# Multi-query attention with a SiLU feed-forward on one core: K of two chunks in two column tiles, two query blocks by the whole array at the loop's start, and another tail

## The chip, the cores and the metric

One core of one Trainium2 chip. TensorE (PE) multiplies, with the weights loaded beside it (PEld); VectorE (DVE), ScalarE (ACT) and GpSimd (POOL) do the element work; SyncE (SP) issues most transfers. Time is the device's, in microseconds, for one execution. The kernel before took 1090.62 us (median of three, 1089.78 to 1091.57).

## The reference

Inputs are 2048 tokens of width 512. 32 query heads of width 16 share one K and one V of width 16. Beside the attention stands a feed-forward of width 1792, and a gate mixes them:

```
q = (x @ wq) in 32 heads;  k = x @ wk;  v = x @ wv
a = softmax(q k^T / 4) v, heads joined, @ wo
b = silu(x @ w1) @ w2
g = sigmoid(sum(x * gate_w))
out = g * a + (1 - g) * b
```

## The kernel before, in words

Each fp32 operand is kept as two fp16 parts (a "split": one copy on ScalarE or VectorE, one subtraction on VectorE), and a product is three matmuls. The first pass does all the work at fixed scales; checks along the way fill `mxs`, and a second, slower pass runs only if a flag is set, which it is not here.

**Prologue** (`first_pass`). The instructions of each engine stand in the order in which the code issues them (a manual schedule), so a late operand holds everything behind it on that engine. `T(c, t)` transposes 128 tokens of chunk c (four matmuls against the identity into a bank `pt`) and splits them into `xs`; there are four chunks of 512 tokens. `K(c)` makes K, V and the gate's sum of one chunk in one bank (twelve matmuls with 64 weight columns). `parts`, `v_rows`, `place`, `V` copy K, keep its largest value, put K into the layout `KT`, and turn V. `W` splits wq, `Q(n)` makes query block n (n = 4 x chunk + o, 128 query columns each) and writes it to DRAM (`qd`), `load_q` reads it back into a tile `qb`, `shift` bounds its scores through `kab` and writes the softmax's shift (`sh`). Query blocks 0 and 1 are made here (`AHEAD` is 2). `Pieces` splits the 37 pieces of w1, wq, w2 and wo, each loaded by a DMA into one of three raw tiles; `step` does one piece.

**Loop** (`attention`). 32 rounds (16 query blocks, two halves each) of 16 key tiles make 512 steps; an iteration takes two steps, s and s + 1. A string of letters says what PE does in it: S is one of four groups of scores (line 977, eight matmuls on 50 rows by 32 columns) followed by one exponential on ScalarE (line 980, 128 x 1024); F is one slot of the product stream; P and N are probabilities times V. In the first of the two steps the probabilities may be split (PPP, with VectorE's two subtractions at line 1001) or native fp32 (N); `low` decides that by `split_step`; the other step is always native. Six F stand in an iteration, twelve in a `WIDE` one, which is taken after a tanh while `debt` is 6 or more.

The product stream (`stream`, `outs`) makes, out by out, the hidden layer (`ffn_h`, whose eviction is a tanh), the later query blocks (`q_block`), the second layer (`ffn_o`) and the output projection (`out_proj`). An out's upper 64 rows of products run beside the lower 64 rows of the next out: a slot holds four 64 x 32 products of each. Banks come from `pM`, of which there are two.

`fill` closes an iteration: from a budget in microseconds less what was spent, it issues work that was put off (`todo`), a weight piece, or a chore. After the last query bound (`open_q` empty), chores gather the checks: `gather` writes `md` to DRAM, `row` reads it back on SP, `check` (line 634) works on it.

**Tail.** After the loop, `plain` sends what is left of the stream through the whole array, 128 x 128, in order, two banks, each out evicted when it is done.

Of the kernel before, what the change touches and what calls it, by code (L numbers as in the profile page):

```python
# [28 lines left out]
FIRST = "SSBSSFFFFFF"  # L29
AHEAD = 2  # L30
# [14 lines left out]
def kernel(  # L45
# [158 lines left out]
    nc.gpsimd.memset(mxs, 0.0)  # L204
    for q in qb_:
        nc.gpsimd.memset(q, 0.0)
    for t_ in (VH, VL, VF):
        nc.gpsimd.memset(t_, 0.0)
    nc.gpsimd.memset(VH[:, :, 16:17], 1.0)
    nc.gpsimd.memset(VF[:, :, 16:17], 1.0)  # L210

    def masks(cst):
# [4 lines left out]
        mj = cst.tile([16, 8, 16], F32)  # L217
        nc.gpsimd.iota(mj, pattern=[[0, 8], [1, 16]], base=0, channel_multiplier=-1, allow_small_or_imprecise_dtypes=True)
        sel_k = cst.tile([16, 8, 16], F32)
        nc.vector.tensor_scalar(flat(sel_k), flat(mj), 0.0, None, op0=OP.is_equal)  # L220
        selA = cst.tile([16, 8, 16], F16)
        selB = cst.tile([16, 8, 16], F16)
        nc.vector.memset(selA, 0.0)
        nc.vector.memset(selB, 0.0)
        for b in (0, 2, 4, 6):
            nc.vector.tensor_copy(selA[:, b], sel_k[:, b])
        for b in (1, 5):
            nc.vector.tensor_copy(selB[:, b], sel_k[:, b])
        part = cst.tile([128, 1], F32)
        nc.gpsimd.iota(part, pattern=[[0, 1]], base=0, channel_multiplier=1, allow_small_or_imprecise_dtypes=True)  # L230
        pm = cst.tile([128, 1], F32)
        nc.vector.tensor_scalar(pm, part, 64.0, -64.0, op0=OP.is_ge, op1=OP.mult)
        nc.vector.tensor_tensor(pm, pm, part, op=OP.add)
        rm = cst.tile([128, 2], F32)
# [5 lines left out]
        hj = cst.tile([128, 32], F32)  # L240
        nc.gpsimd.iota(hj, pattern=[[16, 32]], base=0, channel_multiplier=0, allow_small_or_imprecise_dtypes=True)
# [6 lines left out]
        return sel_k, selA, selB, m_one, hmask  # L248
# [35 lines left out]
    def loads(sb, q_cols):  # L284

        wkr = sb.tile([128, KD, DH], F32)
        nc.scalar.dma_start(wkr, by_row(wk))
        wvr = sb.tile([128, KD, DH], F32)
        nc.scalar.dma_start(wvr, by_row(wv))
        gwr = sb.tile([128, KD], F32)  # L290
        nc.scalar.dma_start(gwr, gate_w.rearrange("(p k) -> p k", k=KD))
        xn = []
        for c in range(NCH):
            t_ = sb.tile([128, 4, D], F32, name=f"xn{c}")
            for a in range(2):
                nc.sync.dma_start(t_[:, 2 * a:2 * a + 2], x[c * 512 + a * 256:c * 512 + a * 256 + 256].rearrange("(t p) d -> p t d", p=128))
            xn.append(t_)
        wqr = sb.tile([128, KD, q_cols], F32)
        nc.sync.dma_start(wqr, by_row(wq)[:, :, :q_cols])
# [4 lines left out]
        nc.gpsimd.tensor_copy(flat(wkv[:, :, 48:49]), gwr)  # L304
        return xn, wqr, wkv
# [17 lines left out]
    def sigmoid(sb, pv_, zsc):  # L323

        ez = sb.tile([128, NKT, 1], F32)
        nc.scalar.activation(ez, pv_[:, :, 16:17], AF.Exp, scale=zsc)
        ez = flat(ez)
        nc.vector.tensor_scalar(ez, ez, 1.0, None, op0=OP.add)
        nc.vector.reciprocal(gg, ez)
        nc.vector.tensor_scalar(g1, gg, -0.5, 0.5, op0=OP.mult, op1=OP.add)  # L330
# [20 lines left out]
    def first_pass():  # L351
        with ExitStack() as pro:
# [3 lines left out]
            sel_k, selA, selB, m_one, hmask = masks(sb)  # L356
            xn, wqr, wkv = loads(sb, 256)
            pieces_ = Pieces(S1, S2, SO, SQ)
            bank = lambda name, bufs: ps.tile([128, 512], F32, name=name, bufs=bufs)
            wkvs = sb.tile([128, 2, KD, 64], F16)  # L360
            vr = sb.tile([64, S], F32)
            mx = sb.tile([16, NCH], F32)
            mxa = sb.tile([16, 1], F32)
# [7 lines left out]
            def K(c):  # L371
                ks[c] = bank("pk", 2)
                kv_product(ks[c], wkvs, c)

            def parts(c):
                pk = ks[c]
                k1, k2 = ks[c, "k"] = [wk_.tile([16, 512], F16, name=n) for n in ("k1", "k2")]
                nc.scalar.activation(k1, pk[0:16], AF.Copy, scale=k_to)
                absmax(mx[:, c:c + 1], k1)
                if c == NCH - 1:  # L380
                    nc.vector.tensor_reduce(mxa, mx, axis=AX.X, op=OP.max)
                nc.vector.scalar_tensor_tensor(k2, pk[0:16], k_to, k1, op0=OP.mult, op1=OP.subtract)

            def v_rows(c):
                nc.scalar.activation(vr[32:64, c * 512:c * 512 + 512], ks[c][32:64], AF.Copy)

            def place(c):
                pk = ps.tile([128, 512], F32, name="pt", bufs=4)
                k_places(pk, *ks[c, "k"], selA, selB)
                nc.scalar.activation(KT[:, c * 512:c * 512 + 512], pk, AF.Identity, bias=m_one)  # L390

            def V(c):
                for t in range(4 * c, 4 * c + 4):
                    nc.tensor.transpose(pv_[:, t], vr[32:64, t * 128:t * 128 + 128], ident[32:64, 32:64])
# [20 lines left out]
            def shift(n, pu):  # L415
# [4 lines left out]
                if n == 0:  # L420

                    for p, queue in enumerate((nc.scalar, nc.sync)):
                        queue.dma_start(qb_[0][48:113:64, p], s1[32 * p:32 * p + 3:2])
                return q_shift(o, c, s1)

            split(wkvs[:, 0], wkvs[:, 1], wkv, SKV)
            for m, a, n in (M_K, 0, 16), (M_V, 32, 16), (M_G, 48, 1):
                absmax(mxs[:, m:m + 1], wkvs[:, 0, :, a:a + n], AX.XY)
            T(0, 0, 1, 2, 3)

            pq = bank("pq", 1)
            pv_ = ps.tile([128, NKT, 32], F32, name="pv")
            T(1, 0, 1)
            K(0)
            T(1, 2, 3)
            T(2, 0)
            parts(0)
            T(2, 1)
            v_rows(0)
            K(1)  # L440
            place(0)
            T(2, 2, 3)
            T(3, 0)
            V(0)
            parts(1)
            T(3, 1)
            v_rows(1)
            W(0)
            W(1)
            K(2)  # L450
            pieces_.step(by_scalar=True)
            pieces_.step(by_scalar=True)
            place(1)
            T(3, 2, 3)
            V(1)
            parts(2)
            for _ in Q(0, pq):
                pass
            load_q(qb_[0], 0, 0, 0, 0)
            v_rows(2)  # L460
            pieces_.step(by_scalar=True)
            K(3)
            parts(3)
            place(2)
            q1 = Q(1, bank("pq", 1))
            next(q1)
            prep = bank("pk", 2)
            nc.tensor.matmul(prep[:, 0:1], flat(sel_k), mxa, start=True, stop=True)
            kv_ = sb.tile([128, 1], F32)
            nc.vector.tensor_copy(kv_, prep[:, 0:1])  # L470
            nc.vector.tensor_scalar(kab, hmask, kv_, 2.0 ** -10 * (1 + 2.0 ** -9), op0=OP.mult, op1=OP.mult)
            v_rows(3)
            place(3)
            note = shift(0, bank("pk", 2))
            pieces_.step(by_scalar=True)
            V(2)
            V(3)
            nc.vector.tensor_copy(VF[:, :, 0:16], pv_[:, :, 0:16])
            v_parts()
            sigmoid(sb, pv_, -1.0 / (SX * SKV))  # L480
            nc.vector.tensor_scalar(g1, g1, 1.0 / (SX * S1 * S2), None, op0=OP.mult)
            nc.vector.tensor_scalar(gg, gg, 1.0 / (SX * SKV * SO), None, op0=OP.mult)

            lo = sb.tile([16, 2], F32)
            nc.vector.tensor_scalar(lo[:, 0:1], mxa, 0.5, None, op0=OP.is_lt)
            nc.vector.tensor_scalar(lo[:, 1:2], mxa, 6e4, None, op0=OP.is_gt)
            nc.vector.tensor_tensor(mxs[0:16, M_KK:M_KK + 1], lo[:, 0:1], lo[:, 1:2], op=OP.max)
# [3 lines left out]
            pieces_.step(by_scalar=True)  # L491

        with ExitStack() as phase:
            attention(phase, lambda c, o: DH ** -0.5 / LAM, 0.5 / (SX * S1), 1, pieces_, list(chores()),
                      list(range(AHEAD, NO * NCH)), [(1, 0, qx)])


    def second_pass():
        with ExitStack() as pro:
# [3 lines left out]
            sel_k, selA, selB, m_one, hmask = masks(sb)  # L503
# [80 lines left out]
            sigmoid(sb, pv_, zsc)  # L584
# [13 lines left out]
        with ExitStack() as phase:  # L598
            phase.enter_context(tc.manual_schedule())
            attention(phase, lambda c, o: esc[:, c * NO + o:c * NO + o + 1], tsc, 2, pieces_, [], [], [])  # L600
# [95 lines left out]
    def attention(ctx, scale_of, t_scale, shifts, split_pieces, chores, q_todo, bounds):  # L696
# [55 lines left out]
        def fill(length):  # L752
# [3 lines left out]
            if bounds and turn[0] and turn[1] == 6 and not turn[0].hidden and len(bounds) > turn[0].is_q:  # L756
# [5 lines left out]
            if split_pieces.left() and (room >= 1.3 or split_pieces.count < 6.6 + 0.6 * cycle[0]):  # L762
# [44 lines left out]
        queue, open_q = [], q_todo + bounds  # L807

        def q_block(n):
# [4 lines left out]
            def evict(pq):  # L814
                q2 = qx.rearrange("p (a b) -> p a b", a=2)
# [3 lines left out]
                qa = wp.tile([128, 512], F32, name="e", bufs=2).bitcast(F16)  # L819
# [287 lines left out]
```

## Time and profile before

| what | us |
|---|---|
| median of three runs | 1090.62 |
| the profiled execution | 1091.79 |
| its span | 1089.8 |
| first score matmul | 41.05 |
| first exponential | 42.84 |
| end of the last exponential | 1068.55 |
| end of the last sum on VectorE | 1084.15 |
| PE / ACT / DVE busy | 1065.3 / 1012.0 / 792.9 |

A row of the timeline has start, duration, engine, line, operation, the tiles written and read, count, and in brackets how long the engine sat idle before it and for whom. A row of the view by stretches has the stretch, its length, the engine's busy time with the instructions touched in brackets, the granted TensorE clock (1.00 is full), the share of the DMA engines and GB/s. A row of a group has its count, its busy time and the mean in ns, and the idle time before.

### The profile page before, as it was taken

How to read it: one execution, taken by the hardware profiler on the slowest of the kernel's cores; microseconds unless marked ns; L12 is line 12 of the kernel's file. 1: busy time of each engine (PE TensorE's matmuls, PEld its weight loads, DVE VectorE, ACT ScalarE, POOL GpSimd, SP SyncE). 2: the span in 40 equal slices, each digit the busy share in tenths (PEclk: the TensorE clock that was granted, in tenths of full speed). 3: DMA queues.
4: the chain of work that ended last, by engine and by line, in shares of the span. 5: the costliest groups of instructions: out<-in, count | busy, mean ns of one | idle time of the engine just before them, and what ended most of it. 6: DMA issues, size and time to landing. Idle time of an engine off the chain costs nothing.

```text
span 1089.8 us, 66260 instructions
## 1 busy us (share of the span) xinstructions
PE 1065.3 (98%) x31366; PEld 700.0 (64%) x31366; DVE 792.9 (73%) x1085; ACT 1012.0 (93%) x1123; POOL 23.5 (2%) x53
## 2 busy tenths in 40 slices
PE   7999999999999999999999999999999998999996
PEld 5355666767665577677755667587756775656652
DVE  5647886978779687878776696776868657675875
ACT  4699999999999999999999999899999998999992
POOL 1110000000000000000000000000000000000000
PEclk9799999999999999999999999999999999999999
DMA  5221211210001000000000100000000101000001
GB/s 205 84 64 38 69 42 40 60 34 21 12 11 40 31 22 7 18 12 11 22 11 21 36 28 12 21 12 12 22 5 20 50 11 21 12 9 7 12 4 43
DMA packets 20841, 32.97 MB, mean 30 GB/s; under 512 B 5137, under 2 KB 12050, under 8 KB 20562
## 3 DMA queue, kind: packets, MB, share of 16 engines
q1 hardware_dynamic: 17614, 20.46, 6.0%
q0 software_dynamic: 2512, 8.13, 2.6%
q8 instruction: 247, 4.05, 1.6%
q14 instruction: 32, 0.26, 0.1%
q10 hardware_dynamic: 436, 0.07, 0.0%
HBM read 20.12 MB, written 8.52 MB: 26 GB/s over the span
## 4 chain that ended last, share of the span: by engine, by line
PE 87%; DVE 7%; ACT 4%; DMA 1%; issue 1%; ACTq 0%; SPq 0%; POOL 0%
PE pv L1023 34%; PE pm L736 31%; PE S L977 19%; ACT P L980 4%; DVE L L1001 3%; DMA md<-raw 1%; PE pm L740 1%; PE pt L310 1%; DMA gwr<-in_gate_w_dram 1%; DVE acc L717 0%; DVE T L924 0%; PE pk L124 0%; PE pk L125 0%; PE pk L126 0%; DVE U L925 0%
## 5 line engine op out<-in xcount | busy, mean ns | idle before, releaser
L980 ACT ACTIVATE P<-S 128x1024 f32<-128x1024 f32 x1024 | 965.6, 1047 | 31.3 <-PE S L977 22.3
L977 PE MATMUL S<-qb,KT 50*32 50x512 f16 x8192 | 491.3, 379 | 2.5 <-ACT P L980 2.5
L1001 DVE TENSOR_TENSOR L<-P 128x1024 f16<-128x1024 f32 x352 | 412.2, 1217 | 10.5 <-ACT P L980 10.4
L1023 PE MATMUL pv<-P,VF 64*32 64x512 f32 x5376 | 377.2, 591 | 0.0
L977 PEld LDWEIGHTS <-KT 50*32 50x32 f16 x8192 | 191.5, 90 | 183.7 <-issue 120.8
L736 PE MATMUL pm<-w2s,H 64*32 64x512 f16 x5184 | 262.1, 375 | 3.8 <-issue 2.7
L736 PE MATMUL pm<-xs,w1s 64*32 64x512 f16 x5376 | 247.6, 377 | 1.0 <-DVE acc L717 0.6
L736 PEld LDWEIGHTS <-H 64*32 64x32 f16 x5184 | 148.9, 93 | 43.8 <-issue 16.3
L736 PEld LDWEIGHTS <-w1s 64*32 64x32 f16 x5376 | 143.0, 93 | 39.8 <-issue 12.7
L1023 PEld LDWEIGHTS pv<-P,VF 64*32 64x32 f32 x5376 | 130.9, 107 | 26.8 <-issue 9.5
L785 DVE SCALAR_TENSOR_TENSOR e<-e,pm 128x512 f32<-128x512 f32 x56 | 38.4, 685 | 141.1 <-ACT e L784 140.0
L736 PE MATMUL pm<-xs,wqs 64*32 64x512 f16 x1344 | 93.2, 375 | 0.0
L1023 PE MATMUL pv<-L,VH 64*32 64x512 f16 x1408 | 84.9, 375 | 0.7 <-DVE L L1001 0.5
L1023 PE MATMUL pv<-P,VH 64*32 64x512 bf16 x1408 | 84.7, 389 | 0.0
L1023 PE MATMUL pv<-P,VL 64*32 64x512 bf16 x1408 | 84.2, 386 | 0.0
L1023 PEld LDWEIGHTS <-VH 64*32 64x32 f16 x2816 | 66.5, 92 | 20.9 <-issue 6.0
L736 PE MATMUL pm<-wo_s,O 64*32 64x512 f16 x1440 | 65.9, 375 | 0.0
L924 DVE STREAM_TRANSPOSE T<-pv 128x512 f32<-128x512 f32 x32 | 22.9, 717 | 54.1 <-PE pv L1023 43.5
L736 PEld LDWEIGHTS <-wqs 64*32 64x32 f16 x1344 | 49.1, 93 | 12.7 <-issue 4.1
L717 DVE SCALAR_TENSOR_TENSOR acc<-pm,g,acc 128x512 f32<-128x512 f32 x48 | 35.7, 744 | 25.3 <-PE pm L736 23.2
L736 PEld LDWEIGHTS <-O 64*32 64x32 f16 x1440 | 34.3, 93 | 13.2 <-issue 2.4
L784 ACT ACTIVATE e<-pm 128x512 f32<-128x512 f32 x56 | 34.4, 615 | 6.3 <-PE pm L736 6.3
(148 smaller groups left out, 491.1 us busy)
## 6 DMA issues: line engine op xcount, KB each, us to landing
qb<-qd SPq DMA_DIRECT2D x192, 32.0 KB
raw<-in_B_w_dram POOLq DMA_DIRECT2D x23, 256.0 KB, 3.0
xn<-in_A_x_dram SPq DMA_DIRECT2D x8, 512.0 KB
out_dram<-acc SPq DMA_DIRECT2D x16, 256.0 KB
qd<-qx SPq DMA_DIRECT2D x14, 256.0 KB
raw<-in_A_wo_dram POOLq DMA_DIRECT2D x4, 256.0 KB, 2.9
qb<-sh SPq DMA_DIRECT2D x62, 2.0 KB
raw<-in_B_w_dram SPq DMA_DIRECT2D x3, 256.0 KB
```

Source lines behind the costliest of these rows:

```text
L310: nc.tensor.transpose(pt[:, kt], xn[c].rearrange("p t (d k) -> p t k d", k=KD)[:, t, kt], ident)
L717: nc.vector.scalar_tensor_tensor(a, po, gate[:, n:n + 1], a, op0=OP.mult, op1=OP.add)
L736: nc.tensor.matmul(self.bank[32 * m:32 * m + 32], l(i, rows, 32 * m), r(j, rows), start=first, stop=last)
L740: nc.tensor.matmul(self.bank, l(i, slice(0, 128), 0, 128), r(j, slice(0, 128)), start=first, stop=last)
L784: nc.scalar.activation(e, ph, AF.Tanh, scale=t_scale)
L785: nc.vector.scalar_tensor_tensor(e, e, 1.0, ph, op0=OP.add, op1=OP.mult)
L924: nc.vector.transpose(T, pv[0])
L977: nc.tensor.matmul(sc[32 * m:32 * m + 32, f], KT[b:b + 50, k0:k0 + 32], qtile[i][b:b + 50, j], start=True, stop=True)
L980: nc.scalar.activation(P[:, 2 * j:2 * j + 2], sc, AF.Exp, scale=scale_of(c, o))
L1001: nc.vector.tensor_tensor(lows[s][:, q], P[:, q], upper(P)[:, q], op=OP.subtract)
L1023: nc.tensor.matmul(pvs[i][h][32 * j:32 * j + 32], a[r], b[r, j], start=first, stop=last)
```

## The change

`K(c)` now makes chunks c and c + 1 together: each of its twelve products is issued twice, into PSUM partitions 0 to 63 and 64 to 127 of one bank. So `parts`, `vr`, the masks and the maximum work on 80 or 128 partitions and twice instead of four times; `V` turns 128 x 128. The identity is made first, the clearing of tiles on POOL comes after the loads, wq is loaded before the last chunk. The prologue's order is new, its weight pieces are two instead of five on ScalarE, and the gates' VectorE part moves into iteration s = 4. This is ScalarE's queue from its start to the loop (`xs` are splits of transposed tokens, `wkvs` of the K, V and gate weights, `KT` is K in place, `qs_` a query block, `w1s` a weight piece). Before:

```order
L115 ACTIVATE wkvs<-wkv 128x256
L115 ACTIVATE xs<-pt 128x4x128 x9
L378 ACTIVATE k_287<-pk 16x512
L115 ACTIVATE xs<-pt 128x4x128
L385 ACTIVATE vr<-pk 32x512
```

Now:

```order
L116 ACTIVATE xs<-pt 128x4x128 x4
L116 ACTIVATE wkvs<-wkv 128x256
L116 ACTIVATE xs<-pt 128x4x128 x8
L116 ACTIVATE wqs<-wqr 128x2x256 x2
L394 ACTIVATE k_321<-pk 80x512
L395 ACTIVATE vr<-pk 128x512
L116 ACTIVATE xs<-pt 128x4x128 x4
L116 ACTIVATE qs__367<-pq 128x512
```

Four token splits now stand ahead of the weights' split, and twelve ahead of the first K copy (ten before).

In the loop, the first iteration has no F. Its string FIRST has 28 letters, and E is one whole-array matmul of query blocks 4 and 5 (`EARLY`): ten before the first scores, fourteen between them. Those two blocks leave the list of the stream. Each is followed by a weight piece. `split_step` asks for a VectorE backlog under 0.8, `fill` hands out pieces at 0.57 an iteration from 5.6 (0.6 from 6.6 before), `debt` starts at 18, and bounds are taken in the order of their blocks, no longer beside a query block's end. This moves the check's read on SP. Before:

```order
L623 DMA md<-raw_80 128x1
L256 DMA qb_83<-qd_3_107 16x2x512
L257 DMA qb_83<-qd_3_107 16x2x512
L258 DMA qb_83<-qd_3_107 16x2x512
L260 DMA qb_83<-sh_3_108 1x2x512
...
L628 DMA raw_81<-md 1x128
```

Now:

```order
L649 DMA md<-raw_80 128x1
L654 DMA raw_81<-md 1x128
L262 DMA qb_84<-qd_3_91 16x2x512
```

The read of `md` stood behind the eight loads of a query tile, and now stands right behind the write; on VectorE three hidden-layer evictions lie between the gather and the check.

In the tail, 18 of the 36 whole-array products of before now lie in the stream. What is left, one `ffn_o` and four `out_proj`, goes into banks that are free by then (two of the scores' tiles are used), the four out by out in turn. VectorE's queue from the last probabilities on. Before:

```order
L931 TENSOR_TENSOR C<-T,rr 128x16x16
L935 STREAM_TRANSPOSE T<-C 128x512
L119 CAST O<-T 128x512
L120 TENSOR_TENSOR O<-T,O 128x512
L717 SCALAR_TENSOR_TENSOR acc<-pm,g_65,acc 128x512
L717 SCALAR_TENSOR_TENSOR acc<-pm,gg,acc 128x512 x4
L717 SCALAR_TENSOR_TENSOR acc<-pm,g_65,acc 128x512 x3
```

Now:

```order
L965 TENSOR_TENSOR C<-T,rr 128x16x16
L743 SCALAR_TENSOR_TENSOR acc<-pm,g_65,acc 128x512
L969 STREAM_TRANSPOSE T<-C 128x512
L120 CAST O<-T 128x512
L121 TENSOR_TENSOR O<-T,O 128x512
L743 SCALAR_TENSOR_TENSOR acc<-S,g_65,acc 128x512
L743 SCALAR_TENSOR_TENSOR acc<-pm,gg,acc 128x512 x2
L743 SCALAR_TENSOR_TENSOR acc<-S,gg,acc 128x512 x2
```

Five sums follow O instead of eight, and one stands ahead of the last transpose (row 841 of VectorE's order).

The diff, cut to its core:

```diff
-FIRST = "SSBSSFFFFFF"
-AHEAD = 2
+FIRST = "EEEEEEEEEESEESEEEESEEEESEEEE"
+AHEAD, EARLY = 2, (4, 5)
...
             def K(c):
-                ks[c] = bank("pk", 2)
-                kv_product(ks[c], wkvs, c)
+                pk = ks[c] = bank("pk", 2)
+                for kt in range(KD):
+                    for n, (i, j) in enumerate(((0, 0), (0, 1), (1, 0))):
+                        for h in range(2):
+                            nc.tensor.matmul(pk[64 * h:64 * h + 64], wkvs[:, i, kt], xs[:, j, kt, (c + h) * 512:(c + h) * 512 + 512],
+                                             start=kt + n == 0, stop=kt == KD - 1 and n == 2)
+                    yield
...
-                    for p, queue in enumerate((nc.scalar, nc.sync)):
-                        queue.dma_start(qb_[0][48:113:64, p], s1[32 * p:32 * p + 3:2])
+                    for p in range(2):
+                        nc.sync.dma_start(qb_[0][48:113:64, p], s1[32 * p:32 * p + 3:2])
...
+            T(0, 0, 1, 2, 3)
             split(wkvs[:, 0], wkvs[:, 1], wkv, SKV)
+            pq = bank("pq", 2)
+            T(1, 0, 1, 2, 3)
+            T(2, 0, 1)
+            k = K(0)
+            next(k)
+            next(k)
+            T(2, 2)
+            next(k)
+            next(k)
+            T(2, 3)
+            W(0)
+            W(1)
+            parts(0)
+            T(3, 0)
+            q0 = Q(0, pq)
+            next(q0)
+            next(q0)
+            T(3, 1)
+            next(q0)
+            next(q0)
+            T(3, 2, 3)
+            next(q0)
+            load_q(qb_[0], 0, 0, 0, 0)
+            place(0)
+            place(1)
+            V(0)
+            k = K(2)
+            for _ in k:
+                pass
+            parts(2)
...
-            if bounds and turn[0] and turn[1] == 6 and not turn[0].hidden and len(bounds) > turn[0].is_q:
+            if bounds and turn[0] and turn[1] == 6 and not turn[0].hidden and not turn[0].is_q:
...
-            if split_pieces.left() and (room >= 1.3 or split_pieces.count < 6.6 + 0.6 * cycle[0]):
+            if split_pieces.left() and (room >= 1.3 or split_pieces.count < 5.6 + 0.57 * cycle[0]):
...
-            return steps[s][1] > 0 and not (turn[0] and turn[0].hidden and (0 < turn[1] <= 6 or wide[0]))
+            return steps[s][1] > 0 and backlog[0] < 0.8 and not (turn[0] and turn[0].hidden and (0 < turn[1] <= 6 or wide[0]))
...
+        def early_products():
+            for n in early:
+                o = q_block(n)
+                o.bank = pM.tile([128, 512], F32, name="pm")
+                for i in range(len(o.mm)):
+                    o.whole(i, i == 0, i == len(o.mm) - 1)
+                    if i < len(o.mm) - 1:
+                        yield
+                o.evict(o.bank)
+                split_pieces.step()
+                yield
...
+            if gates_ and s == 4:
+                gates_()
+                spend(0.6)
...
         plain[0] = True
+        for _ in work:
+            pass
+        bank = lambda: pM.tile([128, 512], F32, name="pm")
+        halves = lambda: (lambda t: [t[:, 0], t[:, 1]])(pS.tile([128, 2, 512], F32, name="S"))
...
+        ends, banks = [], halves()
+        while left[0]:
+            o = next(seq)
+            if o is not None:
+                o.bank = banks.pop(0) if banks else bank()
+                whole([o], range(len(o.mm)))
+                ends.append(o)
         while todo:
             todo.pop(0)[2]()
-        for _ in work:
-            while todo:
-                todo.pop(0)[2]()
+        for o in ends[:1]:
+            o.evict(o.bank)
+        outs_ = [o() for o in urgent]
+        for o, b in zip(outs_, [bank(), bank()] + halves()):
+            o.bank = b
+        whole(outs_, range(2))
+        whole(outs_, range(2, 3 * NO))
+        for o in outs_ + ends[1:]:
+            o.evict(o.bank)
```

More of the change, by code (lines that the diff above doesn't have):

```diff
@@ L375, in parts @@
             def parts(c):
                 pk = ks[c]
[L377 to L385, printed above, removed]
+                k1, k2 = ks[c, "k"] = [wk_.tile([80, 512], F16, name=n) for n in ("k1", "k2")]
@@ new lines, in first_pass @@
+            V(0)
[3 more added lines that the diff above has]
+            parts(2)
+            pieces_.step(by_scalar=True)
+            q1 = Q(1, bank("pq", 2))
+            next(q1)
+            next(q1)
+            prep = bank("pk", 2)
+            nc.tensor.matmul(prep[:, 0:2], flat(sel_k[0:80]), mxa, start=True, stop=True)
+            kv_ = sb.tile([128, 1], F32)
+            nc.vector.tensor_reduce(kv_, prep[:, 0:2], axis=AX.X, op=OP.max)
+            nc.vector.tensor_scalar(kab, hmask, kv_, 2.0 ** -10 * (1 + 2.0 ** -9), op0=OP.mult, op1=OP.mult)
@@ L427, in first_pass @@
+            next(q1)
+            note = shift(0, bank("pk", 2))
+            place(2)
+            place(3)
+            pieces_.step(by_scalar=True)
             for m, a, n in (M_K, 0, 16), (M_V, 32, 16), (M_G, 48, 1):
                 absmax(mxs[:, m:m + 1], wkvs[:, 0, :, a:a + n], AX.XY)
[L429 to L475, printed above, removed]
-            V(2)
-            V(3)
-            nc.vector.tensor_copy(VF[:, :, 0:16], pv_[:, :, 0:16])
+            lo = sb.tile([128, 2], F32)
+            nc.vector.tensor_scalar(lo[:, 0:1], kv_, 0.5, None, op0=OP.is_lt)
+            nc.vector.tensor_scalar(lo[:, 1:2], kv_, 6e4, None, op0=OP.is_gt)
+            nc.vector.tensor_tensor(mxs[:, M_KK:M_KK + 1], lo[:, 0:1], lo[:, 1:2], op=OP.max)
@@ L502, in second_pass @@
             ps = pro.enter_context(tc.tile_pool(name="props", bufs=2, space=PSUM))
-            sel_k, selA, selB, m_one, hmask = masks(sb)
+            identity(sb)
+            sel_k, selA, selB, m_one, hmask, _ = (t[0:16] if n < 3 else t for n, t in enumerate(masks(sb)))
             xn, wqr, wkv = loads(sb, D)
@@ L827, in bound @@
         def bound():
-            o, c, qa = bounds.pop(0)
+            o, c, qa = bounds.pop(min(range(len(bounds)), key=lambda n: bounds[n][1] * NO + bounds[n][0]))
+            shifted.add((o, c))
             ahead.append(next(seq))
@@ L849, in outs @@
                 else:
-                    for _ in range(2):
+                    while any((k - 1, f) not in Hs for f in range(GF[blocks[k - 1][1]])):
                         yield urgent.pop(0)() if urgent else None
@@ L869, in follow @@
             return o
-        seq, ahead, ended, debt = outs(), [], [None], [12]
-        drains = [0]
+        seq, ahead, ended, debt = outs(), [], [None], [18]
+        drains, left = [0], [4 * len(blocks)]
         turn = [None, 0]
@@ L1045, in attention @@
                 slots, order = NATIVE, [(s - 2, 3), (s - 1, 3)]
-            if not s and bounds:
+            if not s and early:
                 slots = FIRST
@@ L1058, in attention @@
                     n_f += 1
-                elif a == "B" and (bound_now() or not s and bounds):
+                elif a == "B" and (bound_now() or s == 4 and bounds):
                     bound()
```

163 lines of the change are left out of this document (98 added, 65 removed).

## The prediction

> **What bounds the kernel now.** The page first: TensorE (PE) is busy for nearly the whole span.
>
> ```profile
> span 1089.8 us, 66260 instructions
> PE 1065.3 (98%) x31366; PEld 700.0 (64%) x31366; DVE 792.9 (73%) x1085; ACT 1012.0 (93%) x1123; POOL 23.5 (2%) x53
> ```
>
> 98% is not 98% of useful work, so I cut the span at the exponentials of line 980, four to a loop iteration. The view by stretches, for that line alone, gives iteration lengths (second column: us; in brackets the exponentials touched).
>
> ```profile
> 42.84:55.47 12.63, 7.84 (x9) 0.59 0.29 85
> 55.47:1064.70 1009.23, 953.88 (x1013) 1.00 0.08 24
> 241.19:244.91 3.72, 3.72 (x6) 1.00 0.04 11
> 77.15:81.26 4.11, 3.75 (x5) 1.00 0.20 62
> 149.70:153.65 3.95, 3.84 (x4) 1.00 0.02 5
> 175.50:180.69 5.19, 3.99 (x5) 1.00 0.20 58
> 132.81:137.54 4.73, 4.01 (x6) 1.00 0.35 118
> 915.67:923.27 7.60, 3.84 (x6) 1.00 0.26 23
> ```
>
> Row by row: the first two iterations take 12.63 us; the next 253 take 1009.23; a split iteration is 3.72, a native one 4.11 with a tanh and 3.95 without, a wide native one 5.19. The last two are outliers, 1.0 and 3.6 us over their kind. PE explains the kinds. Eight 64-row by 32-column products share one slot, 24 of them start 0.65 us before the next kind (0.217 a slot); behind them, from the chain of waits, a split PV (0.67) and a native one (0.86):
>
> ```profile
> 72.94 0.84 PE L736 MATMUL pm<-xs,w1s 64*32 64x512 f16 x24
> 73.59 0.38 PE L977 MATMUL S<-qb,KT 50*32 50x512 f16 x2
> ```
>
> ```profile
> 65.97 0.67 PE pv L1023 x22
> 66.86 0.86 PE pv L1023 x16
> ```
>
> Four score slots, six product slots, a split PV and a native PV make 3.70. So an ordinary iteration is bound by PE at full clock and cannot be shortened without taking slots away. What can go lies before 55.47, in the outliers, and behind the last exponential. The granted clock shows the first of these (stretches of 3.41 us, PE alone; the third number from the right is the clock):
>
> ```profile
> 37.36:40.77 3.41, 3.41 (x10) 0.50 0.37 102
> 40.77:44.18 3.41, 1.58 (x28) 1.00 0.22 83
> 44.18:47.60 3.42, 2.92 (x44) 0.50 0.63 169
> 47.60:51.01 3.41, 3.41 (x48) 0.50 0.13 44
> 51.01:54.42 3.41, 3.41 (x44) 0.50 0.00 0
> ```
>
> The half clock comes back behind a stretch of 1.58 us of work, and stays while products with one half missing leave part of the array unused; four slow stretches lie around the loop's start.
>
> **The prologue, to the first exponential (now 42.84).** Its rows:
>
> ```profile
> 4.91 3.66 PE L310 MATMUL pt<-ident,xn 128*128 128x128 f32 x16 [4.91 <-DMA xn<-in_A_x_dram]
> 7.77 0.42 ACT L115 ACTIVATE wkvs<-wkv 128x256 f16<-128x256 f32 x1 [4.23 <-POOL wkv L304]
> L116 DVE SCALAR_TENSOR_TENSOR xs<-pt,xs 128x512 f16<-128x512 f32 x13 | 8.5, 683 | 6.8 <-ACT xs L115 6.8
> L382 DVE SCALAR_TENSOR_TENSOR k<-pk,k 16x512 f16<-16x512 f32 x4 | 2.7, 668 | 0.0
> 32.58 0.33 SPq L409 DMA_DIRECT2D qd<-qs__415  x1
> 37.80 1.36 ACTq L423 DMA_DIRECT2D qb<-s  x1
> 41.05 0.62 PE L977 MATMUL S<-qb,KT 50*32 50x512 f16 x16
> 42.32 0.61 ACT L192 ACTIVATE w1s<-raw 128x512 f16<-128x512 f32 x1
> ```
>
> The input still sets 4.9, so the earlier identity gives nothing. K now costs 48 slots of 0.217 us (10.4 us). In column tiles of 64 two chunks share a slot: 24 slots, 5.2 us saved if they run side by side, nothing if not. No row shows 64-column tiles paired; the nearest is the eight-tile row above, which does run side by side, so I take 5.2 and keep 0 as the other end. The transposes move ahead of the wkvs activation, which held ScalarE until 7.77.
>
> Step by step for the new order: ten groups of transposes at the cold 0.92 us each (3.66/4) end at 14.1; K 2.6 and three groups of 0.55 at 18.3; VectorE, at 0.68 a split, is through with wqs only at 19.5 to 20.2, so the first Q block runs 19.5 to 22.8 with a group in it and two more groups end at 23.9; its write leaves at 25.8 instead of 32.58, and the q loads behind it as much earlier. Places and V 1.5, K 2.6: 27.9. Then ScalarE's copy 0.6, VectorE's maximum and k2 (0.67 each) and four short ones (some 0.7) to kab, the bound and its shift 1.1: 31.7, and two SP issues of 0.65 in place of ScalarE's 1.36: 33.2, usable 1.9 us later (37.80 + 1.36 to 41.05), 35.1. PE meanwhile has the Q1 remainder, places and V to 33.3, and ten slots of early blocks, 2.15: scores at 35.5, first exponential at 35.9. ScalarE is free by 35.3: it issues no late DMA and converts two weight pieces instead of five, the last of which (42.32) holds 42.84 today. Places where PE thins out (18.3 to 19.5, 29.2 to 31) can bring a half-clock stretch, up to 1.7 us each; I add 0.6. **36.5, a gain of 6.3**; bounds 35.0 (clock up one stretch sooner) and 39.5 (two slow stretches more).
>
> The Trainium skill, "TensorE: Matmul & The Clock Gate" (Part 4), says a transpose does not count as PE work for the clock. Transposes fill the new prologue's first 9 us, so by that rule the clock would come up some 2 us later than I take it. No row here decides it: the clock came up only after K had begun.
>
> **The loop's first two iterations (12.63).** Now PE does there only half-empty slots (one half of a product with no partner). New: 4 score slots and 14 early whole-array slots, 3.9 us, and one native iteration, 3.95. The change of tile shape costs about 0.1 us, from the pitch across it (0.32 from the first row to the second; 0.22 within one shape):
>
> ```profile
> 20.09 0.38 PE L126 MATMUL pk<-xs,wkvs 128*64 128x512 f16 x1
> 20.41 0.39 PE L320 MATMUL pt<-k,selA 16*128 16x512 f16 x1
> 20.63 0.37 PE L321 MATMUL pt<-k,selB 16*128 16x512 f16 x1
> ```
>
> The first iteration changes shape eight times: 0.8. Sum 8.65; one half-clock stretch at even chance adds 0.85. **9.5, a gain of 3.1**; bounds 8.0 and 12.
>
> The Trainium skill, "TensorEngine Tiling (Array Packing)" (Key Properties), says that a change of tiling mode drains the array, and speaks against this mixing; a full drain at each change (0.38 of a product less its 0.22 slot) would make 1.3 of the 0.8.
>
> **The other 253 iterations (1009.23).** The two blocks leave the stream (24 slots) and 18 products of the tail enter it. By the order of both programs, split 160 becomes 153, native 63 becomes 73, wide split 14 becomes 11 (a wide native's 5.19 less the 0.19 between the PVs: 5.0), wide native stays 16: -7 x 3.72 + 10 x 4.0 - 3 x 5.0 = -1.0, which I leave as spare. The outliers matter more. The check's read of md stands behind eight q loads on SP and VectorE waits for it; in the new order nothing stands between:
>
> ```profile
> 923.73 0.37 SPq L628 DMA_DIRECT2D raw<-md  x1
> 925.07 0.37 DVE L634 TENSOR_REDUCE raw<-raw 1x32 f32<-1x128 f32 x1 [4.76 <-DMA raw<-md]
> 133.33 0.84 PE L736 MATMUL pm<-w2s,H 64*32 64x512 f16 x24 [0.57 <-DVE qx L817]
> L1001 DVE TENSOR_TENSOR L<-P 128x1024 f16<-128x1024 f32 x352 | 412.2, 1217 | 10.5 <-ACT P L980 10.4
> ```
>
> That is 3.6 us. The third row is VectorE's lateness while weights are still split (the 4.73 iteration); by the same cut eleven iterations up to 264 us are together 4.0 over their kind. The new condition, no split step with a backlog of 0.8, gives VectorE two of the last row's 1.217 us back in each step that it turns native; I take the 4.0 as gone. **Gain 7.6**; bounds 4 (late again elsewhere) and 9. The gates (four short VectorE rows) move into iteration s = 4, where VectorE is idle; their first user comes some 15 iterations later.
>
> **The tail.** Rows behind the last exponential, and the clock there:
>
> ```profile
> 1056.43 12.12 ACT L980 ACTIVATE P<-S 128x1024 f32<-128x1024 f32 x13
> 1070.57 0.72 DVE L924 STREAM_TRANSPOSE T<-pv 128x512 f32<-128x512 f32 x1 [1.36 <-PE pv L1023]
> 1073.89 0.43 DVE L119 CAST O<-T 128x512 f16<-128x512 f32 x1
> 1074.37 4.79 PE L740 MATMUL pm<-wo_s,O 128*128 128x512 f16 x12 [2.45 <-DVE O L119]
> 1083.40 0.75 DVE L717 SCALAR_TENSOR_TENSOR acc<-pm,g,acc 128x512 f32<-128x512 f32 x1 [0.54 <-PE pm L740]
> 1075.00:1078.20 3.20, 3.05 (x7) 0.50 0.22 82
> ```
>
> Now: 13.6 us from T to the last sum. New: six slots ahead of the last PV put T 0.4 later; one sum in the chain (row 841 of the new VectorE order) 0.75, O at 1075.5; eight products in four banks 1.7, then one product and its latency 0.45 and four sums at VectorE's 0.75: end at 1080.7 at full clock, 1082.6 at half. PE idles 2.2 us in it (2.45 now), so either can come. **Gain 2.5**; bounds 1.5 and 3.5. The 5.6 us from there to the span's end stay.
>
> **Sum.** 6.3 + 3.1 + 7.6 + 2.5 = 19.5: span 1070.3. The profiled execution took 1091.79, 1.99 beside its span, and the median of the runs is 1.17 below it: 1070.3 + 2.0 - 1.2 = **1071.1 us**, 1.8% faster; its own range, 1067 to 1075.
>
> **Rivals.**
> 1. The clock stays half through more of the new start (first exponential 39.5, two iterations 12.0): 14.0 gained, **1076.6**. For: four half-clock stretches there now; against: whole-array products fill what was thin. Chance 0.17. By the Trainium skill's rule on transposes (named above) it would be likelier.
> 2. The 64-column pairs do not run side by side: 5.2 lost again, **1076.3**. Against: the eight-tile row. 0.06.
> 3. VectorE is as late as now in the weight phase, at other places, so that the 7.6 are not had: **1078.7**. 0.08.
> 4. Nothing is gained: PE slots are only moved (3295 of 0.217 and 336 native PVs of 0.86 make 1004 us now, 3256 and 346 make 1004), and PE was the bound already at the start: within 0.2% of **1090.6**. Against: 12.63 us for 8.65 us of work. 0.03.
> 5. Slower. The weight pieces are handed out more slowly (0.57 an iteration for 0.60) while VectorE also serves the early blocks; PE then waits at its product slots for a piece. If each of the 33 pieces in the loop cost 1.0 us, as the 4.73 iteration does, that is +33 - 19.5: **1104**. It decides from 0.6 us a piece. Against: the third row above waits for a bank's eviction, not for a weight. 0.03.
>
> **The numbers.** The forecast has 0.63. Range 1065 to 1079: below, all gains at their upper bounds (7.8 + 4.6 + 9 + 3.5, 1065.7); above, rivals 1 to 3. A difference under 0.2% cannot be told from none here. Faster by more: 0.63 + 0.17 + 0.06 + 0.08 = 0.94; within: 0.03; slower: 0.03.
>
> **What would show it.** First exponential near 36.5; K's 48 products at half the pitch per product; s = 4's first exponential 9.5 us after the first; no iteration of 7.6; the last exponential to the last sum some 13 us (15.6 now). It is wrong if ordinary iterations are no longer 3.7, 4.0 and 5.2, or if the first two still take 12.

## The result: 1071.24 us, and the profile after

The changed kernel takes 1071.24 us (median of four runs, 1070.47 to 1071.37) against 1090.42 (1089.78 to 1091.57): a ratio of 0.9821, 95% interval 0.9804 to 0.9838. The forecast was 1071.1. The sum came out, but its terms did not: three were too small, one was too large and put down to a wrong cause, and one that was taken as unchanged grew by 0.7.

The page, the first rows after:

```profile
span 1069.5 us, 65974 instructions
PE 1047.9 (98%) x31236; PEld 662.3 (62%) x31236; DVE 769.8 (72%) x1064; ACT 1006.2 (94%) x1116; POOL 24.2 (2%) x54
```

The view by stretches for the exponentials' line (now 1015): the first two iterations, the other 253 up to the last one's first exponential, and two single iterations, s = 372 and s = 374. In later rows of this form the busy time is that of the engine in question, ScalarE or TensorE; what is read from them is the length and the clock.

```profile
34.40:43.16 8.76, 7.82 (x9) 1.00 0.48 152
43.16:1047.20 1004.04, 952.26 (x1013) 1.00 0.08 24
779.65:787.75 8.10, 4.04 (x6) 1.00 0.05 4
787.75:793.59 5.84, 3.97 (x5) 1.00 0.01 3
```

| stretch | before | after | gain | forecast |
|---|---|---|---|---|
| to the first exponential | 42.84 | 34.40 | 8.4 | 6.3 |
| first two iterations | 12.63 | 8.76 | 3.9 | 3.1 |
| the other 253 iterations | 1009.23 | 1004.04 | 5.2 | 7.6 |
| last exponential's end to the last sum | 15.60 | 12.03 | 3.6 | 2.5 |
| last sum to the span's end | 5.65 | 6.38 | -0.7 | 0 |

The last iteration itself (3.85 before, 3.89 after) makes up the rest. The clock is full from the prologue to the last sum; the four half-clock stretches around the loop's start are gone. But **the long iteration is not gone**: s = 372 takes 8.10 us, 3.2 over its kind (the median of the iterations with the same letters, 4.9), as s = 434 did before (7.60). The prediction named its cause and expected it gone, so the first four experiments went there.

### The profile page after: what moved, and what is told of

It is laid out like the page before. It is cut to its first block, busy times and chain, and to the rows that moved or that the text cites. A ratio compares the mean times of both kernels' runs of the same rounds, so it can differ in the third digit from the quotient of the medians.

```text
span 1069.5 us, 65974 instructions
## 1 busy us (share of the span) xinstructions
PE 1047.9 (98%) x31236; PEld 662.3 (62%) x31236; DVE 769.8 (72%) x1064; ACT 1006.2 (94%) x1116; POOL 24.2 (2%) x54
## 4 chain that ended last, share of the span: by engine, by line
PE 90%; ACT 4%; DVE 3%; issue 2%; DMA 1%; SPq 0%; POOL 0%; DVEq 0%; POOLq 0%; ACTq 0%
PE pv L1058 36%; PE pm L762 32%; PE S L1012 20%; ACT P L1015 4%; PE pt L317 1%; DVE acc L743 0%; DMA xn<-in_A_x_dram 0%; DVE T L958 0%; PE pk L387 0%; DVE U L959 0%; DMA raw<-in_B_w_dram 0%; DVE T L960 0%; DVE C L965 0%; DMA qd<-qs__367 0%; DMA qb<-qd 0%
## 5 line engine op out<-in xcount | busy, mean ns | idle before, releaser
L1012 PE MATMUL S<-qb,KT 50*32 50x512 f16 x8192 | 478.1, 378 | 2.7 <-issue 1.4
L1036 DVE TENSOR_TENSOR L<-P 128x1024 f16<-128x1024 f32 x332 | 389.4, 1217 | 7.1 <-ACT P L1015 7.1
L1058 PE MATMUL pv<-P,VF 64*32 64x512 f32 x5536 | 383.1, 589 | 0.4 <-issue 0.4
L762 PEld LDWEIGHTS <-H 64*32 64x32 f16 x5328 | 144.6, 93 | 45.8 <-issue 12.7
L762 PEld LDWEIGHTS <-w1s 64*32 64x32 f16 x5376 | 136.2, 93 | 43.8 <-issue 12.5
L762 PE MATMUL pm<-xs,wqs 64*32 64x512 f16 x1152 | 79.7, 375 | 0.0
L1058 PE MATMUL pv<-P,VH 64*32 64x512 bf16 x1328 | 77.6, 389 | 0.0
L1058 PE MATMUL pv<-P,VL 64*32 64x512 bf16 x1328 | 77.2, 385 | 0.0
L1058 PE MATMUL pv<-L,VH 64*32 64x512 f16 x1328 | 76.2, 374 | 0.0
L1058 PEld LDWEIGHTS <-VH 64*32 64x32 f16 x2656 | 56.9, 92 | 18.2 <-issue 2.3
L762 PEld LDWEIGHTS <-wqs 64*32 64x32 f16 x1152 | 41.8, 93 | 11.7 <-issue 3.6
```

The lines of the kernel that those rows point to most:

```text
L762: nc.tensor.matmul(self.bank[32 * m:32 * m + 32], l(i, rows, 32 * m), r(j, rows), start=first, stop=last)
L1012: nc.tensor.matmul(sc[32 * m:32 * m + 32, f], KT[b:b + 50, k0:k0 + 32], qtile[i][b:b + 50, j], start=True, stop=True)
L1036: nc.vector.tensor_tensor(lows[s][:, q], P[:, q], upper(P)[:, q], op=OP.subtract)
L1058: nc.tensor.matmul(pvs[i][h][32 * j:32 * j + 32], a[r], b[r, j], start=first, stop=last)
```

## Experiments: the long iteration

In the timeline of the changed kernel the gather (`md<-raw`) leaves SP at 778.66, ahead of the stall, and TensorE stops in the middle of eight score products, for nothing that the profile shows:

```profile
778.66 0.34 SPq L649 DMA_DIRECT2D md<-raw  x1
786.92 0.23 SPq L654 DMA_DIRECT2D raw<-md  x1
782.98 0.40 PE L1012 MATMUL S<-qb,KT 50*32 50x512 f16 x5
784.78 0.39 PE L1012 MATMUL S<-qb,KT 50*32 50x512 f16 x3 [1.40 <-issue]
786.83 1.94 ACT L1015 ACTIVATE P<-S 128x1024 f32<-128x1024 f32 x2 [2.97 <-remote]
```

Neither `row` (786.92) nor the check had been issued when TensorE stopped, so the check's wait cannot be the cause. The kernel before reads the same way: an issue on SP that takes 0.4 takes 3.00, and right behind it TensorE halts between products.

```profile
916.64 3.00 SPq L257 DMA_DIRECT2D qb<-qd  x1
923.04 0.62 PE L736 MATMUL pm<-w2s,H 64*32 64x512 f16 x11 [2.15 <-issue]
```

What is common to both is in the DMA queues. The page's row for the instruction fetches, then the row of the same queue from 780 to 790 alone, and last the kernel before from 915 to 922 (packets, MB, share of 16 engines):

```profile
q8 instruction: 246, 4.03, 1.6%
```

```profile
q8 instruction: 2, 0.03, 4.1%
```

```profile
q8 instruction: 1, 0.02, 2.7%
```

Over the span a fetch of 16 KB takes 1.6% of 16 x 1069.5 us / 246 = 1.1 us; these two take 4.1% of 160 / 2 = 3.3 each, and the one of the kernel before 2.7% of 112 = 3.0. From this came theory W: the gather's write, 128 pieces of four bytes into DRAM, makes what follows it slow, the instruction fetches among it.

**The same kernel again.**

> The changed kernel once more, nothing edited. In the changed kernel's trace one iteration of the loop, s = 372, took 8.10 us where its kind takes 4.9; the kernel before has one of 7.60. In both, 128 four-byte packets (the gather of the maxima, md<-raw, into DRAM) had gone out 0.6 to 1.6 us ahead of an instruction fetch of 16 KB that took 3.2 and 3.1 us for a median of 1.05. Theory W (the gather's four-byte writes to DRAM make the fetch late, and TensorE runs out of instructions): the long iteration comes again at the same place, within four iterations behind the gather, 3 to 4 us over its kind, and the time is 1071.2. Theory R (a pause of the memory that comes at its own moment): it stands elsewhere or not at all; the time 1067.5 to 1071.5. Theory C (the prediction's: the wait for the check's read of md): as W, but with the long iteration at the check, not ahead of it.

1071.43 us (1070.42 to 1072.21), and the long iteration at the same place; theory R falls:

```profile
780.52:788.54 8.02, 4.04 (x6) 1.00 0.05 4
```

**The gather without the check.** Gather and write stay; the read of the row and the comparisons behind it are left out, and the flag is written as 0.

```
-        return todo, gather, row, *(lambda n=n: check(n) for n in range(0, len(RANGES), 3)), verdict
+        def none():
+            nc.vector.memset(flag, 0)
+
+        return todo, gather, none
```

> Leaves out the read of the gathered row and the comparisons that decide on the second pass (the decision is written as no); the gather and its write to DRAM stay. Theory C (the wait for the check's read): the long iteration goes, 3.6 us less than the changed kernel, 1067.6. Theory W (the gather's write makes instruction fetches late): it stays, 3 to 4 us, near 1071. Theory R (a pause at its own moment): it stands wherever it falls, 1067.5 to 1071.5.

1070.88 us (1070.58 to 1072.55). Without any read of `md`, and so without a wait for one, s = 372 takes 9.25 (a half-clock stretch of 3.4 follows the stall). Theory C, the prediction's, falls.

```profile
779.77:789.02 9.25, 4.63 (x6) 0.87 0.04 4
```

**The gather on the chip.**

```
-            nc.sync.dma_start(md.rearrange("(p o) -> p o", o=1), mr)
+            nc.sync.dma_start(m, mr)
...
-            nc.sync.dma_start(m, md.rearrange("(o p) -> o p", o=1))
+            pass
```

> The gather writes its 128 maxima straight into the row in SBUF that the check reads, with no stop in DRAM; gather, check and decision all stay. Theory W: no iteration is more than 1 us over its kind behind the gather, no instruction fetch of 3 us, and the time falls by 3.2 to 3.9, to 1067.6. Theory C: the check still waits for a DMA, so the long iteration stays, 1071. Theory R: nothing changes on the average, 1071.

1067.10 us (1066.38 to 1068.10), ratio to the kernel before 0.9783 (0.9760 to 0.9806): 4.3 us below the same kernel with the trip through DRAM, on the same chip, with no overlap of the runs. The 253 iterations take 1001.24, for 1004.04 and 1004.40 in the two profiles of the changed kernel. s = 372 and 374 take 5.00 and 5.14, and the fetches from 780 to 790 are back at 2.0% of 160 / 3 = 1.07 us.

```profile
780.81:785.81 5.00, 3.91 (x6) 1.00 0.04 7
785.81:790.95 5.14, 4.00 (x6) 1.00 0.01 3
43.19:1044.43 1001.24, 952.22 (x1012) 1.00 0.09 24
q8 instruction: 3, 0.05, 2.0%
```

**One more such write**, early in the loop, read by nobody:

```
+        todo.insert(0, lambda: nc.sync.dma_start(md..., mxs[:, M_K:M_K + 1]))
```

> One more write of 128 four-byte pieces into the same place in DRAM, issued some hundred iterations earlier, before the maxima are gathered; nothing reads it. Theory W: a second long iteration behind it, 2 to 4 us over its kind with a slow instruction fetch, 1073 to 1075. Theories C and R: no second one, 1071.

1075.37 us (1073.08 to 1076.80), 3.9 more. Behind the extra write (issued at 256.4) the iteration s = 110 takes 6.47; in the changed kernel it takes 4.11. That is 2.4 of the 3.9; the profile has the rest at the gather itself, whose iteration takes 10.89 for 8.10, with the clock at half for 6.8 us. The one fetch between 258 and 262 takes 4.5% of 64 = 2.9 us:

```profile
260.09:266.56 6.47, 4.30 (x7) 1.00 0.02 4
q8 instruction: 1, 0.02, 4.5%
```

**How small is too small?** Three extra writes of 128 pieces each, into places of their own: 16 bytes (at the same place in the program as the extra write above), 64 and 512.

> Three more writes into DRAM, each of 128 pieces and read by nobody, some 8 iterations apart in the stretch from 256 to 350 us: pieces of 16 bytes, of 64 bytes, of 512 bytes. The gather stays. If it is the small piece that makes the memory slow, the 16-byte write is followed by an instruction fetch of 3 us and an iteration 1.5 to 4 us over its kind, the 512-byte one by none, and the 64-byte one tells where between them it turns. If any scattered write does it, all three: 1071.4 + 3 times 2 to 4, 1077 to 1083. If it is four bytes alone: 1071.4.

1071.79 us (1071.52 to 1073.31). None of the three is followed by a slow fetch; behind the 16-byte write s = 110 takes its 4.11, and the fetch there 2.1% of 64 = 1.3 us. The only long iteration is the gather's own.

```profile
259.87:263.98 4.11, 4.11 (x6) 1.00 0.03 8
q8 instruction: 1, 0.02, 2.1%
```

So of the sizes tried only four bytes do it. Open stays whether that comes from the size itself or from how close the pieces lie (sixteen of them in 64 bytes); and which fetch each stop of TensorE waits for, the traces do not show. What they do show is where slow fetches stand: in the twelve profiles with the gather's trip through DRAM one or two fetches behind each four-byte write take 2.3 to 3.7 us; in the two without it, above and below, no fetch in the loop takes more than 2.0. The Trainium skill, "Runtime: NRT & Kernel Launch" (Instruction fetch mechanics) says that the sequencer fetches its next 16 KB block while it runs the current one, and that the cost is mostly hidden; the traces agree where a fetch takes 1.1 us; behind those of 3 us they show stops.

**The same edit in the kernel before.**

> The kernel before, with the one edit that took 4.3 us off the changed kernel: the gather writes its 128 maxima into the row in SBUF, not through DRAM. If the gather's four-byte writes are behind the iteration of 7.60 us there too (theory W), that iteration and its neighbours lose the 4.4 us that they have over their kinds: 1086.0 to 1087. If the wait for the check's read is it in this kernel, where eight q loads stand ahead of the read (theory C, the prediction's), the wait gets shorter by the trip through DRAM but not by the loads: 1088.5 to 1090.4.

1084.52 us, for 1088.93 of the kernel before beside it: ratio 0.9950 (0.9926 to 0.9973). The 253 iterations fall from 1009.23 to 1004.77, and the one that took 7.60 takes 3.96. Theory W holds for both kernels.

```profile
54.99:1059.76 1004.77, 976.30 (x1069) 1.00 0.08 24
915.29:919.25 3.96, 3.85 (x6) 1.00 0.21 53
```

## Experiments: the parts of the change

Beside these runs the kernel before ran between 1084.5 and 1094.9 us, so what is under 2 us is read from the stages of the profiles. "By their kinds" means each iteration set to the median of its kind.

**K's pairs, in another order.** All three products of one chunk, then of the other, for each k position (`for h` outside `for n`).

> K of two chunks in the same two 64-column tiles, but for each of the four k positions all three products of one chunk, then all three of the other, so that only one in three neighbours can pair. If tiles of neighbouring products run side by side only when they alternate, up to two thirds of the 24 shared slots at 0.217 are lost: 16 slots, 3.5 us of TensorE. Half of it stands in the first K, where TensorE later waits 0.73 us for the first weights of Q, half in the second, all of it on the path: 1.0 to 1.7 + 1.7, the first exponential 2.7 to 3.4 later than 34.40, 1074.2. If the hardware finds the pairs itself (product order within the two tiles does not matter): 34.4 and 1071.2. If they do not run side by side at all (the prediction's second rival): no change either, and the 24 products of the second K would take 5.2 us in both; in the changed kernel they took 2.78, so that is ruled out already.

1071.68 us, first exponential 34.05: nothing is lost. The second K takes 2.79 us for 2.78. So the pairs need not be neighbours; three in a row of one tile still run beside the three of the other.

**K chunk by chunk** (`for h` outermost: 12 products of one tile, then 12 of the other).

> K's 64-column products in the same two tiles, all 12 of one chunk and then all 12 of the other, so that no neighbours are of different tiles but at the border. With three in a row of a tile the products still ran side by side. If the array holds only a few products ahead, nothing pairs here: the second K takes near 5.2 us for 2.78, the first one 2.4 more, less the 0.73 that TensorE waits behind it; first exponential 3.5 to 4.3 later than 34.4, 1074.7 to 1075.5. If it looks a dozen ahead, nothing changes: 34.4 and 1071.4.

1076.06 us, first exponential 38.51, 4.11 later; from there on all stages are the changed kernel's. The second K, in the changed kernel and here:

```profile
24.06 2.78 PE L387 MATMUL pk<-xs,wkvs 128*64 128x512 f16 x24
```

```profile
26.41 4.53 PE L387 MATMUL pk<-xs,wkvs 128*64 128x512 f16 x24
```

24 products one by one would take 24 x 0.217 and the rest of the last one, 5.4; at 4.53 some four pairs still form where the tiles meet (an estimate from the 0.87 between the two). Of the 4.1 us, 2.35 come from the first K (the first Q product starts at 20.33 for 17.98) and 1.75 from the second. Without any pair each of the two would cost 2.6 more, 5.2 together, which is the prediction's term; measured are the 4.1.

**Without the early blocks.** They go back into the stream, the loop begins with `"SSBSSFFFFFF"` as before, and three more pieces are converted by ScalarE ahead of it.

> The change without the two blocks by the whole array: they go back into the stream, the loop's first row is the old one, and three pieces of weights are converted by ScalarE ahead of the loop as before. The prediction's theory: the first two iterations go back from 8.76 to 12.0 to 12.6, the clock comes down to half in two or more stretches of 3.41 there, and the first exponential moves by ScalarE's three pieces at 0.6 less what hides, 0 to 1.8. The stream has 24 slots more, 0 to 5.2 by the kinds of iterations. Sum 1074.5 to 1080. Rival, that TensorE's work is only moved: 1071 to 1073, with the first two iterations long and the body shorter by as much.

1090.49 us, ratio 1.0004 (0.9985 to 1.0022): **the whole gain is gone**, far beyond the expected 1074.5 to 1080. The scores are ready at 34.7, but ScalarE waits 3.56 us for a weight piece that has not landed. Its rows, and TensorE's in the next stretches:

```profile
33.94 1.13 ACT L193 ACTIVATE w1s<-raw 128x512 f16<-128x512 f32 x2
38.63 0.63 ACT L193 ACTIVATE w1s<-raw 128x512 f16<-128x512 f32 x1 [3.56 <-DMA raw<-in_B_w_dram]
39.29 3.74 ACT L1017 ACTIVATE P<-S 128x1024 f32<-128x1024 f32 x4
```

```profile
34.96:38.38 3.42, 0.00 (x0) 0.50 0.80 250
41.79:45.20 3.41, 3.41 (x52) 0.50 0.28 82
48.62:52.03 3.41, 3.41 (x46) 0.50 0.11 29
```

TensorE stands idle, its clock falls to half and stays there for 17 us. Against the changed kernel the first exponential is 4.9 later, the first two iterations 4.4 longer, the other 253 7.9 longer (some 4 by their kinds, for 24 slots more; 1.3 to 1.7 at the gather; the rest, some 2.4, lateness) and the end 1.9 later: 19.1 in all.

**The same, with the pieces on VectorE**, so that no exponential waits for a weight:

```
+            for _ in range(3):
+                pieces_.step()
```

> As in the run without the early blocks, but the three pieces of weights ahead of the loop are converted by VectorE, so that ScalarE's exponentials need not wait for a piece that has not landed (there ScalarE waited 3.56 us for one and began at 39.29). If ScalarE's conversions were all that cost there, the first exponential comes at 34.4 to 35 and the first of s = 4 some 12.6 later, at 47.5: 1085.7. If the weights themselves come too late (the last of the first pieces landed at 38.6) and TensorE has nothing else to do until then, the first exponential comes at 34.4 to 35 but that of s = 4 still at 51 to 52.5, and the time is 1089 to 1090.5.

1088.00 us, ratio 0.9986 (0.9965 to 1.0006). The first exponential comes at 33.99, but the third iteration's only at 50.23 (43.16 in the changed kernel, 55.47 before):

```profile
33.99:50.23 16.24, 12.13 (x163) 0.58 0.36 109
```

That is 0.8 under the 51 to 52.5 of the second expectation and far from the 47.5 of the first: ScalarE's conversions were 2.2 us of it, and the lateness of the weights, with the clock that falls meanwhile, the rest.

**The old tail** (products one out at a time in two banks, `debt` from 12).

> The change with the old end: the last products one sum at a time in two banks, the output projection first, and 18 products fewer moved into the loop. The prediction's theory: the last exponential to the last sum 15.0 to 15.6 for 12.03, the body shorter by the 18 products that leave it (three wide iterations made plain, 0 to 3 us), and the last sum to the span's end back from 6.38 to 5.65, because the last four outputs no longer come 0.7 us apart. Together 0 to 2.5 us slower, 1071.2 to 1073.7. Rival, that the tail's gain is a matter of the clock alone (half in the old tail for 3.4 us, 1.6 us of loss): with the clock full by chance, 1071.

1078.17 us, ratio 0.9892 (0.9863 to 0.9921), 7 us slower, more than expected. The last exponential to the last sum takes 17.39. With the new order of the stream nothing is left for TensorE to do ahead of the output projection: it waits 3.91 us (2.45 before), and the clock falls.

```profile
1060.57 1.33 PE L766 MATMUL pm<-wo_s,O 128*128 128x512 f16 x3 [3.91 <-DVE O L120]
1060.76:1064.17 3.41, 3.41 (x9) 0.50 0.00 0
```

The loop is 3.2 longer too, 2.2 of it at the gather, by the half-clock stretch that followed the stall there. So this is an undo of one half of a pair, and does not price the tail alone.

**The old pace of the weights** (no look at the backlog, 6.6 + 0.6).

> The change with the old rule for split steps (no look at the backlog) and the old pace of the weight pieces. The prediction's theory: the early iterations of the weight phase lose what the change gained there, 4.0 us before against 2.3 over their kinds now, so 1.7 or more, and kinds move by some iterations (native 73 back to 63, 0.28 each, 2.8 us the other way): between 1070 and 1073. Rival, that the lateness has another cause (the pieces' loads): the same excess as in the changed kernel, 2.3, and the time within 1 us of the changed kernel's, by the kinds of iterations alone.

1072.13 us. By their kinds the iterations take some 2 us less (65 native for 73), but those up to s = 110 are some 7.3 over their kinds, for some 1.6 in the changed kernel; two of them, 1.9 and 1.0 over:

```profile
47.11:52.70 5.59, 3.85 (x5) 1.00 0.28 79
123.81:128.53 4.72, 4.00 (x5) 1.00 0.37 116
```

VectorE's lateness is real, and the two new rules together take some 5.7 of it away, for some 2 of slots; which of the two does it was not tried. The 253 iterations are 1.2 longer and not some 3.7, since the gather's stall cost 2.3 less in this execution.

## Why the prediction was right, and where not

**The bound** was read rightly: PE at full clock, kinds of 3.7, 4.0 and 5.2 that do not change (by their kinds in the changed kernel the 253 iterations come to some 999.0 before and some 998.2 after), and gains only at the two ends and in the outliers.

**The prologue** was 2.1 too small, and past its bound of 35.0. The step that failed is "ten groups of transposes at the cold 0.92 us each (3.66/4) end at 14.1". They ended at 12.32: the clock came up in the middle of them. The row of the transposes, and two stretches of equal length:

```profile
4.97 7.35 PE L317 MATMUL pt<-ident,xn 128*128 128x128 f32 x40 [4.97 <-DMA xn<-in_A_x_dram]
6.00:7.20 1.20, 1.20 (x8) 1.00 1.05 384
9.50:10.70 1.20, 1.20 (x12) 1.00 1.05 387
```

From start to start a transpose takes 0.213 until 9.5 and 0.12 behind it; the clock's column says 1.00 in both, since the trace's record of the clock only begins at 9.46. At 0.213 throughout the forty would end at some 13.7 (an estimate: 39 times 0.213 and 0.46 for the last one), so of the 1.8 us the clock has some 1.4 and the 0.92, which spreads the longer last one over every group, 0.4. The moment itself varies: in the other eleven runs with this prologue the record begins 2.8 to 6.0 us after the first transpose, always ahead of any other product, and the forty end at 11.9 to 12.7. Before, the transposes broke off for 1.06 at 8.6, and the products came to full pitch only behind 13.24:

```profile
9.62 1.98 PE L310 MATMUL pt<-ident,xn 128*128 128x128 f32 x8 [1.06 <-DVE xs L116]
13.24 0.49 PE L125 MATMUL pk<-xs,wkvs 128*64 128x512 f16 x1
13.57 0.38 PE L126 MATMUL pk<-xs,wkvs 128*64 128x512 f16 x1
```

So transposes alone brought the clock up, here 4.5 us after the first of them. The Trainium skill, "TensorE: Matmul & The Clock Gate" (Part 4), says that they do not count as work for it; this trace disagrees, and the two microseconds that the prediction gave by that rule were not to be paid. What stands behind moved with it: wq's split ended at 19.33 for 19.5 to 20.2, q's write left at 24.64 for 25.8, and the first exponential came at 34.40 for 35.9. That is 1.5 of the 2.1; the other 0.6, set aside for a half-clock stretch, was not needed. (Two issues of 0.65 behind 31.7 make 33.0 and not 33.2; nothing hangs on it, as the sum waits for TensorE's 35.5.) Of the whole 8.4, 4.1 are K's pairs, by the run chunk by chunk; the other 4.3, the new order and the fewer conversions, were not undone by themselves.

```profile
18.05 1.28 DVE L117 SCALAR_TENSOR_TENSOR wqs<-wqr,wqs 128x512 f16<-128x512 f32 x2
24.64 0.33 SPq L432 DMA_DIRECT2D qd<-qs__367  x1
```

**The first two iterations** went as argued, 8.76 against a sum of 8.65 before the 0.85 for the clock, which stayed full. What the prediction did not see is how the terms hang together. It counted the early blocks at 3.1, and K's pairs and the new order at 6.3. Without the blocks the start of the third iteration moves from 55.47 to 50.23 or 52.48 only, with them to 43.16: 7 to 9 of the 12.3 us gained by there come only if TensorE has work that needs no weights. The prediction had the reason in one clause, that the last conversion "holds 42.84 today", but did not carry it into the price of the blocks.

**The 253 iterations** were 2.4 too large. "The check's read of md stands behind eight q loads on SP and VectorE waits for it ... That is 3.6 us" is the step that failed. The wait on VectorE was there, but beside the stall, not ahead of it; the cause is the write of `md`, which the change kept (some 4.4 us over the kinds before, 3.7 after). The lateness of VectorE up to 264 us, taken as 4.0 gone, went from some 3.9 to some 1.6. The spare 1.0 of slots came to 0.8, and smaller outliers gave the rest, some 1.4.

**The tail** was mis-sized by the clock alone: 2.5 lay between a gain of 3.45 at full clock and 1.55 at half; the clock stayed full, and it gained 3.6. But "the 5.6 us from there to the span's end stay" did not hold: it took 6.38. The last four outputs now leave within 2.3 us instead of 7.9, and the DMA engines are full meanwhile (share 1.03, 370 GB/s; the issues before and after, and the stretch after):

```profile
1076.59 7.93 SPq L720 DMA_DIRECT2D out_dram<-acc  x4
```

```profile
1061.17 2.31 SPq L746 DMA_DIRECT2D out_dram<-acc  x4
1062.00:1064.80 2.80, 0.00 (x0) 0.89 1.03 370
```

That this costs the 0.7 is not shown: with the old tail, where the four leave within 7.1 us, the same stretch took 5.99, and in eight other runs with the new tail and the early blocks 5.8 to 6.3.

**From span to time** the prediction added 0.8 (1.99 beside the span, less 1.17); it was 1.74. That took back the 0.8 by which the gains were larger, so that the forecast came out closer than its terms. The terms missed by 2.1, 0.8 and 1.1 on one side and by 2.4, 0.7 and 0.9 on the other; that the sum hit within 0.2 us is luck.

**The rivals.** A clock at half through the start (1) did not come in the changed kernel, but is what the kernel without early blocks shows. Pairs that do not run (2) are refuted by 2.78 us for 24 products. VectorE as late as now (3) came in part, as some 1.6. Nothing gained (4): its time is what the kernel takes without the early blocks, ratio 1.0004. Weights late (5): they did not hold up the changed kernel's loop, but that same run shows what late weights cost where TensorE has nothing else to do.

## What to carry to other kernels

Follow a stall from the engine that sets the end: if it stops in the middle of a row of like instructions for "issue", look at the instruction queue's fetches and at what was written to DRAM just before, not at the next semaphore wait on another engine. Gather small values on the chip, or in pieces of 16 bytes and more; one edit of two lines was worth 4.3 us here, and made 1067.10. Work that needs no weights, put where the weights are still under way, pays twice: for itself, and by the clock that it keeps up.

## What was not expected of the hardware

- One write of 128 four-byte pieces to DRAM makes the next one or two fetches of 16 KB take 2.3 to 3.7 us for 1.1, and costs TensorE 1.5 to 6 us; 16-, 64- and 512-byte pieces do nothing of the kind.
- Transposes alone bring the clock up: in the twelve runs with the new prologue 2.8 to 6.0 us after the first.
- Products of two column tiles pair with three in a row of each tile (2.79 us for 24) and hardly with twelve in a row (4.53). That would fit an array that looks ahead by some four products, an estimate from these two numbers.
